# Earlier picking of the p·V sums, a later p·V of pair 14, and transfers in halves, in a decode kernel of four attention layers

## The chip, the cores and the metric

The kernel runs on one core of a Trainium2 chip. The metric is device time in microseconds (us), the median over repeated executions.

## The reference

Four attention layers for one token, with two sets of weights and caches used in turn (A, B, A, B). Cut to what matters:

```python
# Hq = 32 heads, Sk = 8192 keys, Dh = 192, D = 640, all bf16, one query row
def attn(x, k_cache, v_cache, wq, wo):
    q = (x @ wq).reshape(1, 1, 32, 192).transpose(0, 2, 1, 3)
    scores = einsum("bhqd,bhkd->bhqk", q, k_cache) * 192 ** -0.5
    o = einsum("bhqk,bhkd->bhqd", softmax(scores), v_cache)
    return o.transpose(0, 2, 1, 3).reshape(1, 1, 6144) @ wo

x = A_x
for w in (A, B, A, B):
    x = x + attn(layernorm(x), w.k_cache, w.v_cache, w.wq, w.wo)
```

Every K and V cache is read once per layer. A layer needs 32 heads x 8192 keys x 192 x 2 bytes, 100.7 MB of K and as much of V. So the kernel is one long read of the caches, with just enough arithmetic to keep up, and four places where a layer ends and the next one starts.

## The kernel before

A layer works through 16 pairs of heads. K and V of a pair are 6.29 MB each, that is 128 rows of 49,152 bytes. On chip they go into a pool of 8 slots of 24 KB per partition; a whole K or V takes two slots, a half takes one. All loads but that of the input row are issued by one engine (SP) into one queue, in the order of a list called `plan`; each issue waits until the slots that it overwrites have been read. Two more lists matter: `steps` is the order in which the compute work of a layer is written to the engines, and `released` says at which step a slot becomes free. The slot search takes, for each transfer, the slots that become free earliest in `steps`. So moving a step in the program can move a transfer into another slot.

The steps of pair p have one-letter names, which the text uses:

- `m` (products): VectorE multiplies K by the query row, four operations of 1.7 us for each half of K; TensorE sums them with identity matmuls into PSUM.
- `s` (softmax): maximum and exponentials.
- `v` (p·V): TensorE multiplies V by the exponentials. The result lies in PSUM in eight pieces that have to be picked and added.
- `e` (picking, `gather` in the code): VectorE picks and adds the eight pieces, then TensorE and ScalarE write one row of o.
- `wc`, `wo`, `wob`, `wol`: the output projection. `wc` turns the rows of o of five pairs into columns, `wo` multiplies a block of the weights by them. In layers 1 and 3 the last block comes in two transfers (`NB`, `wob`), and `wol` are the rows of the last pair.
- `wq`: query rows of a layer. In layers 2 and 3 they are loaded in three blocks.

Some caches stay on chip: K of pair 0 of layer 0 is kept for layer 2, and V of pairs 14 and 15 of layer 1 for layer 3.

The order of the steps, as the kernel before has it (cut to the lines that the change touches):

```python
            for p in range(NPAIR):
                ...
                steps.append(("m", l, p, 0))
                ...
                if p == NPAIR - 1:
                    steps.append(("v", l, p - 1))      # p.V of pair 14 between the halves of K15
                steps.append(("m", l, p, 1))
                ...
                if p == NPAIR - 1:
                    steps.append(("e", l, p - 1))
                elif p > 0 and p % PAIRS_W > 0 or p > 2 * PAIRS_W:
                    steps.append(("e", l, p - 1))      # picking of p-1 behind the products of p
                steps.append(("s", l, p))
                ...
                if p < NPAIR - 2:
                    ...
                    steps.append(("v", l, p))
                    if p + 1 in (PAIRS_W, 2 * PAIRS_W):
                        b = (p + 1) // PAIRS_W - 1
                        steps += [("e", l, p), ("wc", l, b)]
                        both(("wo", l, b))             # both: into plan and into steps
            ...
            plan.insert(-2, ("wo", l, 2))
            steps += [("wc", l, 2), ("v", l, p, 0), ("wo", l, 2), ("v", l, p, 1)]
            if NB[l]:                                  # NB = [0, 5, 0, 5]
                both(("wob", l))
            steps.append(("e", l, p))
            both(("wol", l))
```

Which transfers come whole, and how a slot is chosen:

```python
        def whole(kind, l, p):
            if kind == "t":
                return False
            if kind == "k":
                return l < 2 or l == 3 and p > 1
            if p == NPAIR - 1:
                return False
            return l != 2 or p not in (PAIRS_W, 2 * PAIRS_W)
        ...
        i = min(range(0, NSLOT - k + 1, 2 if k == 2 else 1),
                key=lambda i: (max(end[i:i + k]), first * i))   # the slots released earliest
```

The picking:

```python
            def gather(p):
                ...
                for i in range(2 if end else VK):      # VK = 8; end: pair 15 has two pieces
                    e = DV.op(lambda v, i=i: (
                        v.tensor_scalar(acc[:], O[:, 0:DH], pick[:, 0:1], None, ALU.mult) if i == 0 else
                        v.scalar_tensor_tensor(out=acc[:], in0=O[:, i * DH:(i + 1) * DH], scalar=pick[:, i:i + 1],
                                               in1=acc[:], op0=ALU.mult, op1=ALU.add)), ...)
```

## Time and profile before

The time before is 1990.04 us, the median of 4 runs (1989.65 to 1991.7).

| what | before |
|---|---|
| span of the profiled execution | 1988.6 us |
| bytes of the load queue | 848.38 MB, 99.3% of 16 DMA engines' span |
| TensorE, VectorE busy | 65%, 60% |
| rate in undisturbed stretches | 432 GB/s |

These lines are from the profile page of the kernel before. The first is the span; the second gives the data rate in 40 equal slices of the span (about 50 us each); the last two are DMA queues, with packets, megabytes and the share of 16 engines' span.

```profile
span 1988.6 us, 14015 instructions
GB/s 411 439 428 431 437 430 430 436 430 428 436 429 436 423 431 436 427 434 430 424 393 435 427 428 434 428 430 430 431 403 430 434 431 435 429 438 428 432 436 342
q1 hardware_dynamic: 25712, 848.38, 99.3%
q8 instruction: 45, 0.74, 0.1%
```

The load queue is nearly always busy, so the kernel is bound by its loads. Slices 21 and 30 (393 and 403 GB/s) are dips, and the first and last slices are start and tail.

The windows of the kernel before show the dips at closer range. The columns are named in the first line: stretch, its length, busy time of each engine with the number of instructions, the TensorE clock that was granted, the share of the DMA engines, and GB/s.

```profile
core 0: us, PE busy (x) PEld busy (x) DVE busy (x) ACT busy (x) POOL busy (x), PEclk, DMA share, GB/s
500.00:985.00 485.00, 306.08 (x1963) 36.85 (x768) 283.59 (x323) 32.65 (x108) 0.55 (x1) 0.76 1.00 432
985.00:1010.00 25.00, 19.14 (x198) 4.89 (x122) 15.16 (x19) 1.89 (x7) 0.00 (x0) 0.84 0.92 379
1010.00:1045.00 35.00, 24.38 (x212) 5.87 (x121) 21.96 (x28) 3.85 (x8) 0.55 (x1) 0.79 1.01 410
1470.00:1512.00 42.00, 29.45 (x283) 8.84 (x206) 17.20 (x23) 2.15 (x8) 0.00 (x0) 0.74 0.93 395
1960.00:1989.00 29.00, 19.82 (x265) 8.78 (x210) 10.44 (x20) 2.15 (x8) 0.00 (x0) 0.72 0.67 285
```

The stretch 500 to 985 us is the plateau. Layer 1 ends and layer 2 begins in the second and third window; layer 2 ends in the fourth; the last is the tail.

The next lines are the timeline of the load queue in the kernel before: start in us, time that the issues took, the line of the program, and what is loaded. `x2` are two issues that the view has merged.

```profile
990.10 9.64 SPq L358 DMA_DIRECT2D pool<-in_B_v_cache_dram  x2
1002.03 0.33 SPq L337 DMA_DIRECT2D rows<-in_B_wo_dram  x1
1029.28 0.34 SPq L358 DMA_DIRECT2D pool<-in_A_k_cache_dram  x1
1037.24 0.33 SPq L356 DMA_DIRECT2D pool<-in_A_v_cache_dram  x1
1488.89 0.80 SPq L358 DMA_DIRECT2D pool<-in_A_v_cache_dram  x2
```

The first line is V of pair 15 in layer 1, whose first half is issued at 990.10 us. The last block issued before it landed at 994.5 us, so at that moment the queue holds 4.4 us of work. The second line is `wol` of layer 1. The third is the first K of layer 2 (pair 1), the fourth its first V. The fifth is V of pair 15 in layer 2: it is issued at 1488.89, just when the p·V step of pair 14 has ended (the timeline has the last matmuls of that step at 1488.25 and 1488.69), and the load before it landed at 1489.3: the queue has run dry.

Why V15 is late in layer 1 shows on VectorE, in the timeline of the kernel before:

```profile
976.26 3.14 DVE L622 SCALAR_TENSOR_TENSOR acc<-OY,small,acc 128x192 f32<-128x192 f32 x7
981.41 13.43 DVE L530 TENSOR_TENSOR pool<-pool,q_sb 128x3072 bf16<-128x3072 bf16 x8
995.54 3.13 DVE L622 SCALAR_TENSOR_TENSOR acc<-OY,small,acc 128x192 f32<-128x192 f32 x7
```

The first line is the picking of pair 13, the second the products of K15, the third the picking of pair 14. The products of K15 stand behind softmax of pair 14 in VectorE's program, and that stands behind the picking of pair 13.

The tail of the kernel before, from its timeline:

```profile
1978.90 2.73 PE L593 MATMUL OY<-pool,p_sb 128*4 128x384 bf16 x32 [3.40 <-DMA pool<-in_B_v_cache_dram]
1981.56 0.38 PE L608 MATMUL TB<-small,ones 128*64 128x1 f32 x4
1981.87 1.16 PE L500 MATMUL OY<-oT,pool 128*128 128x1 bf16 x25
1985.36 0.35 SPq L687 DMA_DIRECT2D out_dram<-x_bf  x1
```

TensorE waits 3.40 us for V15's second half, then has 2.73 us of p·V, the sums of the exponentials, and the last block of the projection. The output is issued at 1985.36.

### The profile page before, as it was taken

How to read it: one execution, taken by the hardware profiler on the slowest of the kernel's cores; microseconds unless marked ns; L12 is line 12 of the kernel's file. 1: busy time of each engine (PE TensorE's matmuls, PEld its weight loads, DVE VectorE, ACT ScalarE, POOL GpSimd, SP SyncE). 2: the span in 40 equal slices, each digit the busy share in tenths (PEclk: the TensorE clock that was granted, in tenths of full speed). 3: DMA queues.
4: the chain of work that ended last, by engine and by line, in shares of the span. 5: the costliest groups of instructions: out<-in, count | busy, mean ns of one | idle time of the engine just before them, and what ended most of it. 6: DMA issues, size and time to landing. Idle time of an engine off the chain costs nothing.

```text
span 1988.6 us, 14015 instructions
## 1 busy us (share of the span) xinstructions
PE 1287.4 (65%) x8310; PEld 156.0 (8%) x3266; DVE 1196.8 (60%) x1371; ACT 139.4 (7%) x461; POOL 4.4 (0%) x22
## 2 busy tenths in 40 slices
PE   3566566667466666566675675675667766666667
PEld 0001001000100100100020010010002001001001
DVE  3466575577157566566754575665764764755656
ACT  0000000000000000000010000000000100000000
POOL 0000000000000000000000000000000000000000
PEclk9787787777587688787777777878877877878777
DMA  9999999999999999999999999999999999999998
GB/s 411 439 428 431 437 430 430 436 430 428 436 429 436 423 431 436 427 434 430 424 393 435 427 428 434 428 430 430 431 403 430 434 431 435 429 438 428 432 436 342
DMA packets 25919, 849.26 MB, mean 427 GB/s; under 512 B 3072, under 2 KB 3072, under 8 KB 3840
## 3 DMA queue, kind: packets, MB, share of 16 engines
q1 hardware_dynamic: 25712, 848.38, 99.3%
q8 instruction: 45, 0.74, 0.1%
q14 instruction: 18, 0.15, 0.0%
q10 hardware_dynamic: 144, 0.00, 0.0%
HBM read 848.36 MB, written 0.00 MB: 427 GB/s over the span
## 4 chain that ended last, share of the span: by engine, by line
DMA 65%; DVE 18%; PE 14%; issue 2%; ACT 1%; SPq 0%
DMA pool<-in_B_k_cache_dram 28%; DMA pool<-in_A_k_cache_dram 19%; DVE pool L530 14%; DMA pool<-in_A_v_cache_dram 14%; PE S L58 5%; PE OY L58 4%; DMA pool<-in_B_v_cache_dram 4%; PE OY L593 3%; DVE acc L622 2%; DMA pool<-in_A_wq_dram 1%; DVE s_sb L552 1%; ACT p_sb L567 1%; PE OY L500 0%; PE S L543 0%; DVE acc L621 0%
## 5 line engine op out<-in xcount | busy, mean ns | idle before, releaser
L530 DVE TENSOR_TENSOR pool<-pool,q_sb 128x3072 bf16<-128x3072 bf16 x512 | 861.6, 1753 | 577.0 <-DMA pool<-in_A_k_cache_dram 288.0
L58 PE MATMUL S<-pool,ident 128*128 128x512 bf16 x2944 | 791.0, 426 | 19.2 <-DVE pool L530 17.3
L543 PE MATMUL S<-pool,ident 128*128 128x512 bf16 x128 | 62.6, 489 | 316.4 <-DVE pool L530 316.4
L593 PE MATMUL OY<-pool,p_sb 128*16 128x512 bf16 (+1 forms) x1216 | 156.2, 541 | 128.2 <-DMA pool<-in_A_v_cache_dram 59.4
L58 PE MATMUL OY<-pool,p_sb 128*16 128x512 bf16 x1920 | 219.1, 547 | 0.0
L622 DVE SCALAR_TENSOR_TENSOR acc<-OY,small,acc 128x192 f32<-128x192 f32 x424 | 177.2, 418 | 14.9
L633 PE MATMUL TB<-acc,small 128*1 128x192 f32 x240 | 58.7, 375 | 134.8 <-DVE acc L622 134.8
L489 ACT ACTIVATE q_sb<-QM 128x192 bf16<-128x192 f32 x60 | 19.8, 330 | 1353.2 <-PE QM L483 1353.2
L552 DVE TENSOR_REDUCE s_sb<-S 128x64 f32<-128x512 f32 x128 | 83.4, 683 | 14.7 <-PE S L58 14.6
L617 DVE RECIPROCAL small<-TB 1x2 f32<-1x2 f32 x64 | 11.2, 175 | 109.8 <-PE TB L604 56.7
L543 PEld LDWEIGHTS S<-pool,ident 128*128 128x128 bf16 x128 | 12.9, 101 | 741.5 <-DVE pool L530 679.2
L593 PEld LDWEIGHTS OY<-pool,p_sb 128*16 128x16 bf16 (+1 forms) x1216 | 37.9, 114 | 332.6 <-issue 225.7
L644 ACT ACTIVATE rows<-TB,small 1x192 bf16<-1x192 f32 x120 | 43.1, 405 | 293.5 <-PE TB L633 272.1
L567 ACT ACTIVATE p_sb<-s_sb,small 64x128 bf16<-64x128 f32 x128 | 55.7, 435 | 55.7 <-DVE small L561 54.2
L557 PE MATMUL QM<-ident,m_bf 128*64 128x64 bf16 x128 | 15.1, 233 | 40.6 <-DVE m_bf L554 39.7
L500 PE MATMUL OY<-oT,pool 128*128 128x1 bf16 x900 | 38.2, 178 | 2.2 <-ACT oT L515 2.2
L500 PEld LDWEIGHTS OY<-oT,pool 128*128 128x128 bf16 x900 | 37.1, 131 | 5.4 <-ACT oT L515 2.9
L483 PEld LDWEIGHTS QM<-rows,one_b 1*64 1x64 bf16 x120 | 6.2, 100 | 350.6 <-issue 344.7
L633 PEld LDWEIGHTS TB<-acc,small 128*1 128x1 f32 x240 | 16.3, 87 | 176.6 <-DVE acc L622 143.6
L561 DVE TENSOR_REDUCE small<-QM 128x1 f32<-128x64 f32 x64 | 14.4, 225 | 23.9 <-PE QM L557 23.6
L621 DVE TENSOR_SCALAR acc<-OY,small 128x192 f32<-128x192 f32 x64 | 26.7, 417 | 1.9
L567 ACT ACTIVATION_READ_ACCUMULATOR p_sb<-s_sb,small 64x1 f32 x128 | 23.3, 182 | 0.0
(59 smaller groups left out, 182.6 us busy)
## 6 DMA issues: line engine op xcount, KB each, us to landing
pool<-in_B_k_cache_dram SPq DMA_DIRECT2D x30, 6144.0 KB, 35.9
pool<-in_A_v_cache_dram SPq DMA_DIRECT2D x28, 6144.0 KB, 25.7
pool<-in_B_v_cache_dram SPq DMA_DIRECT2D x28, 6144.0 KB, 29.5
pool<-in_A_k_cache_dram SPq DMA_DIRECT2D x16, 6144.0 KB, 32.9
pool<-in_A_k_cache_dram SPq DMA_DIRECT2D x30, 3072.0 KB, 20.5
pool<-in_A_v_cache_dram SPq DMA_DIRECT2D x8, 3072.0 KB, 13.2
pool<-in_A_wo_dram SPq DMA_DIRECT2D x6, 2400.0 KB, 20.7
pool<-in_B_v_cache_dram SPq DMA_DIRECT2D x4, 3072.0 KB, 24.9
```

Source lines behind the costliest of these rows:

```text
L58: return t.add_instruction(mybir.InstMatmult(name=t.bass.get_next_instruction_name(), engine=mybir.EngineType.PE, ins=[t.lower_ap(rhs), t. ...
L489: lambda a: a.activation(q_sb[i][:], QM[:, 0:DH], ACT.Copy), e, last["q"][i], bank=QMu)
L500: e = PE.op(lambda t, i=i, c=c, f=y_first[0], fin=n[0] == "wol" and i == k - 1: t.matmul(YB[:, c:c + 1], lhsT=t3[:, i, c:D:DC], rhs=o[:, i ...
L530: e = DV.op(lambda v, d0=d0: v.tensor_tensor(k3[:, :, d0:d0 + QD], kin[:, :, d0:d0 + QD], q_sb[qi][:, d0:d0 + QD].unsqueeze(1).broadcast_t ...
L543: t.matmul(S[:, :], lhsT=ident[:], rhs=k3[:, :, d0:d0 + R], start=True, stop=fin) if d0 == 0 else
L552: lambda v, u=u: v.tensor_reduce(s[:, u * JU:(u + 1) * JU], SP_[u][:].rearrange("p (j r) -> p j r", r=R), AX.X, ALU.add), ev_S[p, u], last ...
L567: ev_p[p] = AC.op(lambda a, h=h, r=r: a.activation(p_sb[par][r, :, h], s[r, :], ACT.Exp, bias=negm[par][r, 0:1], accum_out=l_col[par][r, h ...
L593: t.matmul(o, lhsT=x, rhs=y, start=f, stop=fin) if c == 0 else
L621: v.tensor_scalar(acc[:], O[:, 0:DH], pick[:, 0:1], None, ALU.mult) if i == 0 else
L622: v.scalar_tensor_tensor(out=acc[:], in0=O[:, i * DH:(i + 1) * DH], scalar=pick[:, i:i + 1], in1=acc[:], op0=ALU.mult, op1=ALU.add)), e if ...
L633: e = PE.op(lambda t, h=h: t.matmul(TB[96:97, C_O + h * DH:C_O + (h + 1) * DH], lhsT=half[:, h:h + 1], rhs=acc[:], start=True, stop=True), ...
L644: last["TO"] = last["row_written"] = AC.op(lambda a, h=h: a.activation(orow[:, o0 + h * DH:o0 + (h + 1) * DH], TB[96:97, C_O + h * DH:C_O ...
```

## The change

Its intent is to take the picking off VectorE's way to the next softmax, and to issue loads earlier at the places where the queue runs dry. It has five parts:

1. Picking of a pair directly behind its p·V.
2. p·V of pair 14 behind both halves of the products of pair 15, its picking behind softmax 15. In layer 2 the slot search then gives V15's first half another slot.
3. The first V of layer 2 in halves, and its first half ahead of K of pair 1 in the plan.
4. K in halves behind the `wo` blocks (pairs 5 and 10 of layers 0 and 1).
5. In layers 1 and 3, the last half of V15 in two transfers, the sums of the exponentials (called l columns below) ahead of p·V, and `wc` behind the first half of V15's p·V.

The diff, cut to its core; the repeated declaration of semaphores, and the code that merely moves the l columns up, are left out:

```diff
             if kind == "k":
-                return l < 2 or l == 3 and p > 1
+                return l < 2 and p not in (PAIRS_W, 2 * PAIRS_W) or l == 3 and p > 1
             ...
-            return l != 2 or p not in (PAIRS_W, 2 * PAIRS_W)
+            return l != 2 or p not in (0, PAIRS_W, 2 * PAIRS_W)
 ...
-                if p == NPAIR - 1:
-                    steps.append(("v", l, p - 1))
+                if l == 2 and p == 1:
+                    steps.append(("e", l, 0))
                 steps.append(("m", l, p, 1))
 ...
                 if p == NPAIR - 1:
-                    steps.append(("e", l, p - 1))
-                elif p > 0 and p % PAIRS_W > 0 or p > 2 * PAIRS_W:
-                    steps.append(("e", l, p - 1))
+                    steps.append(("v", l, p - 1))
                 steps.append(("s", l, p))
 ...
                             i = plan.index(("k", l, 1, 0))
-                            plan[i - 2:i + 1] = [("k", l, 1, 0)] + plan[i - 2:i]
+                            plan[i - 1:i + 1] = [("k", l, 1, 0), ("v", l, 0, 1)]
                     steps.append(("v", l, p))
+                    if l != 2 or p > 0:
+                        steps.append(("e", l, p))
                     if p + 1 in (PAIRS_W, 2 * PAIRS_W):
                         b = (p + 1) // PAIRS_W - 1
-                        steps += [("e", l, p), ("wc", l, b)]
+                        steps.append(("wc", l, b))
                         both(("wo", l, b))
 ...
-            steps += [("wc", l, 2), ("v", l, p, 0), ("wo", l, 2), ("v", l, p, 1)]
+            steps.append(("e", l, p - 1))
+            steps += [("v", l, p, 0), ("wc", l, 2)] if NB[l] else [("wc", l, 2), ("v", l, p, 0)]
+            steps += [("wo", l, 2), ("v", l, p, 1)]
             if NB[l]:
+                plan.append(("vq", l))
                 both(("wob", l))
 ...
+                if quarters(n):                      # the last half of V15, layers 1 and 3
+                    x = TS // 2
+                    if n in landed:
+                        return SP.op(lambda s: s.dma_start(t[:, x:], r[:, TS + x:]), sem=semVQ, inc=16)
+                    return SP.op(lambda s: s.dma_start(t[:, 0:x], r[:, TS:TS + x]), *free, sem=semS[i], inc=16)
 ...
-                PE.wait(ev_p[p], last["O"])
+                PE.wait(ev_p[p])
+                if 0 in us:
+                    ...                              # the l columns, formerly behind p.V
+                PE.wait(last["O"])
 ...
+                    if p == NPAIR - 1 and i == rounds // 4 and quarters(("v", nl, np_, u)):
+                        PE.wait(need(("vq", l)))
```

More of the change, by code (lines that the diff above doesn't have):

```diff
@@ L168, in build @@
         semS = [sem(f"semS{i}") for i in range(NSLOT)]
-        semOL, semOB, semX, semOUT = sem("semOL"), sem("semOB"), sem("semX"), sem("semOUT")
+        semOL, semOB, semVQ, semX, semOUT = [sem(n) for n in ("semOL", "semOB", "semVQ", "semX", "semOUT")]
         e = PO.op(lambda g: g.memset(ident[:], 0.0))
@@ L305, in build @@
                 before[n] = [("wc", n[1], 2)]
-            elif n[0] == "wob":
+            elif n[0] in ("wob", "vq"):
                 before[n] = []
@@ L328, in wq_rows, with quarters @@
             return slot[place[("wq", l, g)]][:, 0:k * QC].rearrange("p (c n) -> p c n", c=k)
+        def quarters(n):
+            return n[0] == "v" and n[2:] == (NPAIR - 1, 1) and NB[n[1]] > 0
         def transfer(n):
@@ L347, in transfer @@
                     sem=semOB, inc=16)
+            if n[0] == "vq":
+                n = ("v", l, NPAIR - 1, 1)
             i = place[n]
@@ L577, in values @@
                 N = min(512, k * DH)
-                PE.wait(ev_p[p], last["O"])
+                PE.wait(ev_p[p])
+                if 0 in us:
+                    PE.wait(last["rl"])
+                    if p < NPAIR - 1:
+                        e = PE.op(lambda t: t.matmul(TB[96:97, C_L:C_L + 2], lhsT=ones[:, 0:1], rhs=l_col[par][:],
+                                                     start=True, stop=True), bank=TBu)
+                    else:
+                        for h in range(2):
+                            e = PE.op(lambda t, h=h: t.matmul(TB[64 * h:64 * h + 64, C_L:C_L + 1], lhsT=ones[:, 0:1].broadcast_to([P, 64]),
+                                                              rhs=l_col[par][:, h:h + 1], start=True, stop=True),
+                                      signal=h == 1, bank=TBu)
+                    last["lc"][par] = ev_l[p] = e
+                PE.wait(last["O"])
                 rounds = J // k // G
@@ L601, in values @@
                         freed[("v", nl, np_, u)] = e
-                PE.wait(last["rl"])
-                if p < NPAIR - 1:
-                    e = PE.op(lambda t: t.matmul(TB[96:97, C_L:C_L + 2], lhsT=ones[:, 0:1], rhs=l_col[par][:],
-                                                 start=True, stop=True), bank=TBu)
-                else:
-                    for h in range(2):
-                        e = PE.op(lambda t, h=h: t.matmul(TB[64 * h:64 * h + 64, C_L:C_L + 1], lhsT=ones[:, 0:1].broadcast_to([P, 64]),
-                                                          rhs=l_col[par][:, h:h + 1], start=True, stop=True),
-                                  signal=h == 1, bank=TBu)
-                last["lc"][par] = ev_l[p] = e
             def gather(p):
```

## The prediction

> **What bounds it.** The DMA engines. The page's queue table has the one load queue at 99.3% of 16 engines' span, 848.4 MB. By windows, DMA share is 1.00 at 430 to 432 GB/s in the long stretches (0-500, 500-985, 1060-1470, 1512-1960 us), which is the plateau: whole-pair transfers move at about 432.6 GB/s. The Trainium skill ("DMA: Bandwidth & Descriptors", Specifications) gives 435 GB/s as fabric ceiling; the trace agrees closely. DVE (60%) and PE (65%) have slack. At the plateau 848.4 MB take about 1961 us (estimate), so of 1988.6 us only some 27 us are start, tail and holes.
>
> **Where the holes are** (windows, and the queue's waits against the landings before): 985-1060 us runs at 398 GB/s (about 6 us lost), 1470-1512 at 395 (3.6 us), and behind layer 1's wo blocks (670, 820 us) about 1.1 us. Layers 0 and 3 have none.
>
> **What the change does, costed:**
>
> 1. Picking behind p.V. It is eight DVE operations, 0.42 us each, 3.55 us with the reciprocal. It leaves the path K products -> softmax -> p.V and goes into DVE's wait for K (10 us in layers 0/1). On the plateau this is worth nothing: the queue is backed up by 12 us and more. It pays at the end of layer 1: K15's products start 3.8 us sooner (now 981.4 after the picking at 975.6), so V15's first half is issued at about 986 instead of 990.1, when the queue still has work; its second half is no longer issued 2.65 us before the queue runs dry. Worth 2.2 us.
> 2. V(14) after both product halves in the program. In layer 2 the slot search then gives V15's first half the slot of K15's second half, free at about 1477, not V14's, free at 1488.9. The queue ran dry at 1489. Worth 3.0 us.
> 3. Layer 2's first V in halves, with the kept K's slots first: V no longer waits for the last wq block (issued 1037.2 with 1.5 us of work left). Worth 1.75 us. The hole before it (wq's last block, products of half 0; 1.3 us) stays.
> 4. K in halves behind wo: the first half takes a slot free already, margin 4.7 -> over 10 us. Worth 1.1 us in layer 1, nothing in layer 0 (no hole there).
> 5. V15's last half in two: behind the last landing 16 p.V matmuls instead of 32 (2.73 us); the l columns (0.3 us) go ahead. The last wo rows then set the pace, so the tail shrinks by about 1.0 us, once, in layer 3; in layer 1 it starts layer 2 sooner.
> 6. Cost: halves move at 430.2 instead of 432.6 GB/s: 0.4 us.
>
> Layer 3 has 20 us and more queued, so what is gained earlier arrives at the end.
>
> Sum: 2.2+3.0+1.75+1.1+1.0-0.4 = 8.6 us. **Predicted 1981.5 us, 1978.5 to 1986.0 in 8 of 10.** Faster by over 2%: 0; within: 0.99; slower: 0.01.
>
> **In the profile.** Right: bytes, DVE and PE busy times unchanged; slice rates near 393 and 403 GB/s rise above 415; window 1470-1505 at 425 or more; first slices unchanged; from the last V landing to the end 1 us less. Step 1 is wrong if V15's first half in layer 1 is still issued within 5 us of the queue's end; step 2 if a wait of the load queue on p.V of pair 14 still leaves a hole; step 3 if layer 2's first V waits for wq.
>
> **What would make it wrong.** DVE waiting in order for p.V (5.1 us at the lower clock) before K's products: in layer 2 they start about 1.7 us later; if margins of 9 to 12 us are eaten, new holes come. A new hole at layer 2's start, where wq's blocks follow one another. Or engines' skew (up to 4.7 us) that returns as loss.

## The result and the profile after

The kernel after takes 1985.61 us, the median of 4 runs (1985.17 to 1986.01). The ratio to the kernel before is 0.9976, with a 95% interval of 0.9959 to 0.9993. A ratio is the mean time of one kernel's runs over that of the other's of the same rounds, so it is not quite the ratio of the medians. The gain is 4.4 us by the medians. A second measurement of the same kernel, below, gave a ratio of 0.9971.

The page of the kernel after, the same lines as before:

```profile
span 1984.0 us, 13908 instructions
GB/s 412 438 430 431 431 437 429 431 430 431 433 435 431 432 429 436 430 431 432 427 388 433 430 430 430 432 430 430 431 431 427 435 432 434 430 432 432 432 431 353
q1 hardware_dynamic: 26720, 848.38, 99.5%
```

The bytes are the same. The dip of slice 30 has gone (403 before, 431 now). The dip of slice 21 has not: 393 before, 388 now.

The windows of the kernel after, with the columns as before:

```profile
500.00:985.00 485.00, 299.06 (x1975) 35.09 (x776) 288.28 (x325) 32.86 (x109) 0.55 (x1) 0.76 1.00 432
985.00:1010.00 25.00, 18.58 (x207) 5.65 (x142) 12.09 (x18) 1.89 (x7) 0.00 (x0) 0.82 0.95 395
1010.00:1045.00 35.00, 26.61 (x226) 5.53 (x111) 17.32 (x24) 3.86 (x8) 0.55 (x1) 0.74 0.95 391
1470.00:1512.00 42.00, 28.40 (x289) 10.17 (x222) 14.99 (x31) 2.15 (x8) 0.39 (x1) 0.69 1.00 424
1960.00:1989.00 29.00, 15.09 (x235) 8.53 (x199) 5.39 (x16) 2.15 (x8) 0.00 (x0) 0.67 0.56 230
```

(The rate is a mean over the 16 DMA engines.) Before, the 25 us at the end of layer 1 ran at 379 GB/s and the 35 us at the start of layer 2 at 410. Now they run at 395 and 391. Worked out, the 60 us carry 23.8 MB before and 23.6 MB after. As a mean of the engines the hole has not been closed; it has moved by 25 us. In the fourth row, at the end of layer 2, the rate rises from 395 to 424, and that gain stays.

The load queue's timeline after:

```profile
987.05 0.33 SPq L371 DMA_DIRECT2D pool<-in_B_v_cache_dram  x1
1006.66 0.33 SPq L343 DMA_DIRECT2D rows<-in_B_wo_dram  x1
1029.60 0.34 SPq L371 DMA_DIRECT2D pool<-in_A_v_cache_dram  x1
1478.96 10.08 SPq L371 DMA_DIRECT2D pool<-in_A_v_cache_dram  x2
```

V15's first half is issued at 987.05 instead of 990.10, as intended. But the first load of layer 2's caches (now a half of V) starts at 1029.60, against 1029.28 before. At the end of layer 2, V15's first half is issued at 1478.96, ten microseconds sooner than before.

VectorE at the end of layer 1, after:

```profile
978.17 13.43 DVE L543 TENSOR_TENSOR pool<-pool,q_sb 128x3072 bf16<-128x3072 bf16 x8
996.95 3.14 DVE L639 SCALAR_TENSOR_TENSOR acc<-OY,small,acc 128x192 f32<-128x192 f32 x7
```

K15's products start 3.2 us sooner (978.17, was 981.41), now with no picking ahead of them: that of pair 13 has gone. The picking of pair 14 stood behind them before too (995.54); it is now behind softmax 15 as well, at 996.95.

The tail after:

```profile
1968.70 2.73 PE L620 MATMUL OY<-pool,p_sb 128*4 128x384 bf16 x32
1974.80 2.73 PE L620 MATMUL OY<-pool,p_sb 128*4 128x384 bf16 x32
1977.74 1.16 PE L513 MATMUL OY<-oT,pool 128*128 128x1 bf16 x25 [0.21 <-DMA pool<-in_B_wo_dram]
1981.22 0.35 SPq L704 DMA_DIRECT2D out_dram<-x_bf  x1
```

p·V of V15 no longer ends the chain: the projection that follows waits 0.21 us for the second transfer of the last block of wo (`wob`), and from there to the output is 3.5 us.

### Where the time went, as a ledger

The following table is worked out from the DMA records of the traces, in the program's order of transfers; it is not a view of the profile. It cuts an execution at fixed points: (a) the last `wo` block of layer 1 issued ahead of V15 has landed; (b) from there until the `wol` rows of layer 1 have landed; (c) until the first packet of the first K or V transfer of layer 2; (d) until the first `wo` block of layer 2 has landed; (e) until the last one has; (f) until the last `wq` block of layer 3 has; (g) until the last load; (t) from there to the end of the span.

```
                       a      b      c       d       e      f       g     t    span
before              994.5  18.61  17.11  139.60  319.49  50.60  441.60  7.07  1988.6
after               995.1  17.77  17.74  138.88  319.09  47.86  442.01  5.58  1984.0
after, second time  994.5  17.78  17.51  139.24  318.94  47.89  441.94  6.16  1984.0
only V14            994.0  18.03  17.89  140.09  318.84  48.00  442.66  8.21  1987.7
only picking        994.3  20.25  17.13  142.16  319.17  50.53  441.53  6.86  1991.9
only last half      993.9  19.39  18.68  140.81  319.88  49.49  441.82  5.97  1989.9
V14 and last half   994.4  19.32  16.82  141.14  318.84  48.11  442.55  7.58  1988.8
picking put back    994.3  19.13  19.35  138.96  319.24  47.94  442.75  8.16  1989.8
wc first            994.4  17.82  17.37  140.26  318.53  48.70  441.99  5.97  1985.0
K whole             994.1  17.81  17.37  139.66  318.62  48.28  441.53  6.31  1983.7
first V whole       994.4  17.79  17.39  139.88  318.94  48.00  441.66  5.92  1984.0
warm                994.5  17.80  16.98  139.10  319.11  47.71  441.87  5.99  1983.1
products first      994.5  17.79  16.62  142.56  319.14  48.14  441.57  5.58  1985.9
products, wc first  994.5  17.81  15.44  142.93  318.81  48.04  441.61  5.55  1984.7
```

The first two rows give the result: of 4.6 us, 2.7 come from the end of layer 2 (f) and 1.5 from the tail (t). The end of layer 1 (b) gives 0.8, the start of layer 2 (c) takes 0.6 back. One execution of each kernel stands in each row, so differences of a few tenths should not be read. The two largest terms hold in the other rows too: f is 49.5 to 50.6 us in the three rows without V14's move and 47.7 to 48.7 in the eleven with it.

### The profile page after: what moved, and what is told of

Its sections match the earlier page's. It is cut to its first block, busy times and chain, and to the rows that moved or that the text cites. A ratio compares the mean times of both kernels' runs of the same rounds, so it can differ in the third digit from the quotient of the medians.

```text
span 1984.0 us, 13908 instructions
## 1 busy us (share of the span) xinstructions
PE 1273.4 (64%) x8310; PEld 150.1 (8%) x3266; DVE 1200.7 (61%) x1371; ACT 139.5 (7%) x461; POOL 4.5 (0%) x22
## 4 chain that ended last, share of the span: by engine, by line
DMA 68%; DVE 15%; PE 15%; ACT 1%; issue 0%; SPq 0%
DMA pool<-in_B_k_cache_dram 27%; DMA pool<-in_A_v_cache_dram 20%; DMA pool<-in_A_k_cache_dram 14%; DVE pool L543 13%; PE S L58 6%; PE OY L58 5%; DMA pool<-in_B_v_cache_dram 4%; PE OY L620 3%; DMA pool<-in_B_wo_dram 2%; ACT p_sb L580 1%; DVE acc L639 1%; DMA pool<-in_A_wq_dram 1%; DVE s_sb L565 1%; PE OY L513 0%; PE S L556 0%
## 5 line engine op out<-in xcount | busy, mean ns | idle before, releaser
L58 PE MATMUL S<-pool,ident 128*128 128x512 bf16 x2944 | 789.1, 425 | 20.3 <-DVE pool L543 19.0
L650 PE MATMUL TB<-acc,small 128*1 128x192 f32 x240 | 82.1, 493 | 219.1 <-DVE acc L639 219.1
L58 PE MATMUL OY<-pool,p_sb 128*16 128x512 bf16 x1920 | 197.0, 485 | 0.0
L620 PE MATMUL OY<-pool,p_sb 128*16 128x512 bf16 (+1 forms) x1216 | 147.5, 497 | 62.7 <-DMA pool<-in_A_v_cache_dram 56.4
L565 DVE TENSOR_REDUCE s_sb<-S 128x64 f32<-128x512 f32 x128 | 88.1, 688 | 69.4 <-PE S L58 69.4
L595 PE MATMUL TB<-small,ones 128*1 128x2 f32 x120 | 11.4, 165 | 74.1 <-ACT p_sb L580 74.1
## 6 DMA issues: line engine op xcount, KB each, us to landing
pool<-in_B_k_cache_dram SPq DMA_DIRECT2D x28, 6144.0 KB, 38.1
```

The source lines that it names most:

```text
L58: return t.add_instruction(mybir.InstMatmult(name=t.bass.get_next_instruction_name(), engine=mybir.EngineType.PE, ins=[t.lower_ap(rhs), t. ...
L565: lambda v, u=u: v.tensor_reduce(s[:, u * JU:(u + 1) * JU], SP_[u][:].rearrange("p (j r) -> p j r", r=R), AX.X, ALU.add), ev_S[p, u], last ...
L620: t.matmul(o, lhsT=x, rhs=y, start=f, stop=fin) if c == 0 else
L650: e = PE.op(lambda t, h=h: t.matmul(TB[96:97, C_O + h * DH:C_O + (h + 1) * DH], lhsT=half[:, h:h + 1], rhs=acc[:], start=True, stop=True), ...
```

## The experiments

Twelve runs were made, one of them of the kernel after again, all with five rounds, all correct within the reference's tolerance. The kernel before: medians 1991.57, 1990.72, 1991.06 and 1991.44 us. It scatters more than the kernel after: 1988.62 to 1996.02 in 36 executions.

Two theories stood against each other after the first reading:

- **Theory A, the last engine.** A transfer is split over 16 DMA engines, and it has landed when the last of them is done. I had counted a hole in the queue as the mean idle time of the 16. If the engines are spread out in time, a short hole idles those in front and not the last one, and costs little.
- **Theory B, the late `wc`.** The change puts `wc` of layers 1 and 3 behind V15's first half. `wol` is then issued at 1006.66 instead of 1002.03. This opens a new hole that eats the gain.

The expectations of the first two runs below also call "theory B" the prediction's own reckoning, that every hole is worth its mean over the engines.

The spread can be read from the DMA records. The first and the last engine finish the last `wo` block of layer 1 at 990.57 and 994.52 us before, and at 988.34 and 995.07 after. The Trainium skill ("DMA: Bandwidth & Descriptors", section "Why a DMA increments its semaphore by 16 and not by 1") says that a transfer runs on up to 16 engines that finish independently, and that only the full count of 16 means that all data has landed. The trace agrees: the spread at that block is 4.0 us before and 6.7 after, and yet the block's landing moves by no more than 1.2 us over all 14 profiled executions (993.9 to 995.1).

### Each part alone

**Only V14's move** (part 2). Edit of the kernel before:

```diff
-                if p == NPAIR - 1:
-                    steps.append(("v", l, p - 1))
                 steps.append(("m", l, p, 1))
                 if p == NPAIR - 1:
-                    steps.append(("e", l, p - 1))
+                    steps.append(("v", l, p - 1))
 ...
             plan.insert(-2, ("wo", l, 2))
+            steps.append(("e", l, p - 1))
             steps += [("wc", l, 2), ("v", l, p, 0), ("wo", l, 2), ("v", l, p, 1)]
```

> The kernel before with one part of the change: V14's p.V stands behind both product halves of pair 15 and its picking behind that softmax. Theory A (a hole in the load queue costs only what it costs the DMA engine that is last; engines are up to 4 to 7 us apart): the hole at the end of layer 2 (1489 us) reached all engines, so this part alone gives 2.5 to 3.5 us. Theory B (every hole is worth its mean over the engines, as in the prediction): 3.0 us as well; this run does not part them, it sizes the term. V15's first half in layer 2 should be issued about 10 us before the queue runs dry instead of 0.4.

Measured: 1989.68 us (1989.28 to 1991.04), ratio 0.9989 (0.9975 to 1.0002): about 2 us, not quite clear of the noise. The ledger's column f falls from 50.6 to 48.0 us, as it was meant to: V15's first half of layer 2 is issued at 1481.68, 7 us ahead of the end of the queue. But the tail grows from 7.07 to 8.21 us. The move puts the picking of pair 14 behind softmax 15, in front of p·V of pair 15, and at the end of a layer nothing hides it.

**Only the picking** (part 1), for pairs up to 13:

```diff
+                if l == 2 and p == 1:
+                    steps.append(("e", l, 0))
                 steps.append(("m", l, p, 1))
 ...
-                elif p > 0 and p % PAIRS_W > 0 or p > 2 * PAIRS_W:
-                    steps.append(("e", l, p - 1))
 ...
                     steps.append(("v", l, p))
+                    if l != 2 or p > 0:
+                        steps.append(("e", l, p))
 ...
```

> The kernel before with the picking moved directly behind p.V and nothing else. Prediction (theory B): 2.2 us from the end of layer 1. Theory A: at most 0.5 us, because the engine that was last had no hole there, and the start of layer 2 is timed by its own chain (first wq block landed, query row, products of the kept K, slot free at about 1029 us).

Measured: 1993.65 us (1989.57 to 1995.22), ratio 1.0004 (0.9991 to 1.0016): nothing. V15's first half in layer 1 is issued at 987.24, as forecast. Its second half is issued at 1000.88, when only 0.7 us is left in the queue, and column b is 20.25 instead of 18.61 us. In this order p·V of pair 14 stands between the two halves of K15's products on TensorE, so the sums of the second half, which free that slot, still wait for V14. One wait was taken away and the next one took its place. It even cost something: TensorE now stood idle for 3.87 us before p·V of pair 14, and the step took 4.5 us (991.08 to 995.56) instead of 2.8; the clock record has half the clock granted from 991.2 to 994.6, and the full clock at that place in the kernel before.

**Only the last half in two** (part 5 without the move of `wc`); the edit is the `quarters`, `vq` and l-column lines of the diff above.

> The kernel before with V15's last half in two transfers in layers 1 and 3 and the l columns ahead of p.V. Both theories: 1.0 to 1.5 us less, all of it between the last landing and the end; time from the last p.V landing to the end about 1.4 us shorter in the profile.

Measured: 1991.3 us (1989.67 to 1992.49), ratio 0.9993 (0.9981 to 1.0006). In the profile the tail is 5.97 us instead of 7.07, so the 1.0 us of the forecast is there. In the times it does not show: b and c together are 38.1 us here and 35.7 in the kernel before. Whether that is scatter or an effect of this part, one profile can't say.

**V14's move and the last half together**, that is the first and third of these edits in one kernel:

> The kernel before with only two of the parts: V14 behind both product halves, and the tail (V15's last half in two, l columns ahead). Theory A: these two carry the gain, 3 to 4 us below before. Theory B: the other three parts (picking, K in halves, first V in halves) add their 5 us, so it stays 4 to 5 us short of after, that is at before.

Measured: 1988.0 us (1987.67 to 1990.65), ratio 0.9989 (0.9976 to 1.0001). By the medians that is 3.1 us below the kernel before, by the means 2.4. The profiled execution was the slowest of the five, so its span (1988.8) is not typical. This is short of the whole change (0.9971 to 0.9976), though the intervals overlap. It suggests that some part that is missing here matters, although picking alone is worth nothing.

### One part taken out of the kernel after

**`wc` first again:**

```diff
-            steps += [("v", l, p, 0), ("wc", l, 2)] if NB[l] else [("wc", l, 2), ("v", l, p, 0)]
+            steps += [("wc", l, 2), ("v", l, p, 0)]
```

> The kernel after with the wo columns put back ahead of V15's first half in layers 1 and 3 (as the kernel before had it). Theory B: the change lost its gain at the end of layer 1 to this later place (wq of layer 2 issued at 1007.0 instead of 1002.4 us), so about 1.5 to 2 us faster than after. Theory A: only engines that are ahead idle there, so within 0.5 us of after, although wq's issue moves back to about 1003 us.

Measured: 1986.55 us (1985.55 to 1986.78), ratio 0.9970 (0.9957 to 0.9982), the same as the kernel after. These are the two windows of this kernel at the end of layer 1 and the start of layer 2, columns as before:

```profile
985.00:1010.00 25.00, 19.02 (x217) 5.89 (x158) 11.97 (x18) 1.89 (x7) 0.00 (x0) 0.86 0.99 417
1010.00:1045.00 35.00, 25.37 (x214) 5.15 (x99) 17.31 (x24) 3.85 (x8) 0.55 (x1) 0.76 0.95 387
```

Here the hole at the end of layer 1 is closed: 417 GB/s, against 395 after and 379 before. And it gains nothing. The start of layer 2 falls only from 391 to 387, and the 60 us carry 24.0 MB, against 23.6 after and 23.8 before; but the 0.4 MB, worth about 1 us, do not reach the time: column b of the ledger, which goes by the last engine, is 17.82 us here and 17.77 after. Theory B forecast 1.5 to 2 us for this run and is not borne out as the reason for the missing microseconds of the kernel after.

**K whole behind wo** (part 4 out):

```diff
-                return l < 2 and p not in (PAIRS_W, 2 * PAIRS_W) or l == 3 and p > 1
+                return l < 2 or l == 3 and p > 1
```

> After, with K behind the wo blocks of layers 0 and 1 whole again. Prediction and theory B: 1.1 us slower than after (the holes at 673 and 826 us come back, about 0.5 us of idle time as mean of the engines). Theory A: within 0.5 us of after, because the engine that is last (4 to 6 us behind the first) has no hole there, and what is saved there is lost at the start of layer 2.

Measured: 1985.5 us (1985.02 to 1987.42), ratio 0.9971 (0.9957 to 0.9984). The kernel after in the same rounds:

> The kernel after, unchanged, as the reference for the runs of this call on the same chip. 1985 to 1987 us.

It took 1985.84 us (1984.57 to 1987.57), ratio 0.9971 (0.9959 to 0.9984). So no gain of K in halves shows. The intervals alone, about 2.6 us to either side, could not exclude the 1.1 us of the forecast, but the records show why there is none. K of pair 5 in layer 1 is issued 4.7 us before the last engine is done with the block before it, and its first packet follows the issue by 0.96 us; the engines are spread over 4.1 us at that point. The leading engine does stand idle for a while: from its end of the block before to its end of K it takes 15.3 us. The last one takes 14.54 us for the same 6.29 MB, which is 432.7 GB/s, as on the plateau. After this block the spread is smaller, 3.3 us, and the loss is no loss at all. Theory A holds here.

**First V of layer 2 whole** (part 3 out):

```diff
-            return l != 2 or p not in (0, PAIRS_W, 2 * PAIRS_W)
+            return l != 2 or p not in (PAIRS_W, 2 * PAIRS_W)
 ...
-                            plan[i - 1:i + 1] = [("k", l, 1, 0), ("v", l, 0, 1)]
+                            plan[i - 2:i + 1] = [("k", l, 1, 0)] + plan[i - 2:i]
```

> After, with layer 2's first V whole and behind wq's last block again. Prediction and theory B: 1.75 us slower than after. Theory A: 0.3 to 1 us slower, as the hole behind it reaches all engines but costs what is left after the one before it; and more scatter from run to run, since the kernels with a whole V there (before 1990 to 1996 us, picking alone 1990 to 1995) scatter and after (1984.6 to 1987.6) does not.

Measured: 1987.16 us (1985.51 to 1990.93), ratio 0.9982 (0.9970 to 0.9995), against 0.9971 and 0.9976 of the kernel after. The profiled execution has the same span as the kernel after, 1984.0. In the ledger's column d the six kernels with the first V whole have 139.6 to 142.2 us, and the six with halves and the order of the kernel after 138.9 to 140.3. This kernel's own 139.88 stands against 138.88 and 139.24 of the two profiles of the kernel after. But two other kernels with halves have 140.26 and 139.66, on either side of it, and the intervals of the runs overlap. So a gain from the halves is not shown; if there is one, it is about a microsecond.

**Picking put back behind the next pair's products** (part 1 out, the rest in):

```diff
                 if p == NPAIR - 1:
                     steps.append(("v", l, p - 1))
+                elif (p > 0 and p % PAIRS_W > 0 or p > 2 * PAIRS_W) and (l, p) != (2, 1):
+                    steps.append(("e", l, p - 1))
 ...
                     steps.append(("v", l, p))
-                    if l != 2 or p > 0:
-                        steps.append(("e", l, p))
                     if p + 1 in (PAIRS_W, 2 * PAIRS_W):
                         b = (p + 1) // PAIRS_W - 1
-                        steps.append(("wc", l, b))
+                        steps += [("e", l, p), ("wc", l, b)]
```

> After, with the picking back behind the next pair's products; everything else of the change stays. Prediction for this part: 2.2 us slower than after (V15's first half in layer 1 issued at about 991 us again). By subtraction from the runs so far (two parts alone 2.4 us below before, all five 5.0 to 5.6, K in halves 0, first V in halves about 1.5) some 1 to 1.5 us are left for it. Theory A in its strict form says 0.5 us at most, since the last engine's landing at the end of layer 1 is the same in all kernels so far (994 to 995 us for the last wo block).

Measured: 1992.01 us (1989.12 to 1992.65), ratio 1.0002 (0.9988 to 1.0015). Theory A in its strict form said that the picking is worth at most half a microsecond, because the last engine hardly had a hole. Instead the whole gain is gone, and the interval does not touch that of the kernel after in its measurement of five rounds (0.9959 to 0.9984). The picking that was worth nothing when it was added alone cannot be taken out. (Both are compared through the kernel before.)

The lines of this kernel's timeline, first VectorE and the queue at the end of layer 1 (picking 13, products of K15, picking 14, `wol`), then TensorE and the queue in the tail:

```profile
975.98 3.13 DVE L639 SCALAR_TENSOR_TENSOR acc<-OY,small,acc 128x192 f32<-128x192 f32 x7
981.13 13.43 DVE L543 TENSOR_TENSOR pool<-pool,q_sb 128x3072 bf16<-128x3072 bf16 x8
999.91 3.13 DVE L639 SCALAR_TENSOR_TENSOR acc<-OY,small,acc 128x192 f32<-128x192 f32 x7
1009.51 0.33 SPq L343 DMA_DIRECT2D rows<-in_B_wo_dram  x1
```

```profile
1974.28 2.73 PE L620 MATMUL OY<-pool,p_sb 128*4 128x384 bf16 x32
1980.37 2.73 PE L620 MATMUL OY<-pool,p_sb 128*4 128x384 bf16 x32
1986.52 0.35 SPq L704 DMA_DIRECT2D out_dram<-x_bf  x1
```

Picking 14 in layer 1 runs at 999.91, in the kernel after at 996.95; `wol` is issued at 1009.51 against 1006.66; the first transfer of layer 2 has its first packet at 1032.75 against 1030.58. A delay of 3 us runs down one chain of compute and comes out at the other end as 2.2. In the tail, p·V of V15's first half starts at 1974.28 against 1968.70: 2.6 us after its data had landed here, 0.3 us in the kernel after. The last load lands at 1981.64, but p·V ends at 1983.1: the tail is bound by compute now, and takes 8.16 us instead of 5.58. The difference of the two spans, 5.8 us, is 2.6 us of tail, 2.2 us at layer 2's start (its first packet), and 1.0 us in small sums over the rest.

My reading is that the moves belong together. V14's move frees a slot in layer 2, at the price of one picking behind softmax 15 at the end of every layer. Moving the other picking away from in front of K15's products pays that price. But there is a rival. This kernel also has `wc` late, and the kernel with V14 and the last half alone, which kept 2 to 3 us without the picking's move, has not; that one loses less at layer 2's start (column c, 16.82 against 19.35). The two timelines show the difference: there `wol` is issued at 1006.95; here p·V of V15's first half stands ahead of `wc` for 2.7 us, and `wol` is issued at 1009.51. So the late `wc` may be what the picking has to make room for, but no run has tested this by itself.

### What sets the start of layer 2

Column b has a floor. In all eight kernels with picking and V14's move together it is 17.77 to 17.82 us. Between (a) and the `wol` rows the queue moves 6.29 + 0.82 + 0.49 = 7.60 MB; in 17.8 us that is 427 GB/s, as much as rows of this size were seen to get. The kernel before needed 18.61. So by the last engine only 0.8 us was ever to be had at the end of layer 1, and all of it was won. What follows is column c, about 17 us from there to layer 2's first transfer, and the change does not make it shorter. Two things run in it. One is a chain of compute: the projection, the sum over the row, the query row, the products of K0, and their sums, which free the slot. The other is the queue itself: in this time it moves the three `wq` blocks, 7.37 MB, and these alone take about 17.3 us (an estimate from the 426 GB/s at which rows of 11,520 bytes moved in these traces). So column c is nearly all transfer as well. What the chain of compute costs can be bounded: from the `wol` rows to the landing of the first half of layer 2's caches the kernel after takes 26.1 us in both profiles and the kernel before 25.6, while the transfers alone need about 24.6 (the same estimate, with 430 GB/s for the half). So about 1.5 us are lost there after and 1.0 us before, in single executions; the rest of the dip in the windows is idle time of the leading engines.

This is TensorE in the timeline of the kernel after, at that place:

```profile
1020.28 0.59 PE L481 MATMUL OY<-pool,xb 128*1 128x512 bf16 x3 [2.21 <-DMA pool<-in_A_wq_dram]
1023.98 5.59 PE L58 MATMUL S<-pool,ident 128*128 128x512 bf16 x23
1029.50 0.38 PE L481 MATMUL OY<-pool,xb 128*1 128x512 bf16 x3
```

TensorE waits for the first block of `wq` until 1020.28 (1020.60 before), spends 3.3 us on query rows, then 5.6 us on the sums of K0's first half, and at 1029.60 the slot is free and the transfer is issued. Three runs tried to shorten this.

**Products first:** the sums of K0's first half ahead of the query rows, and the last `wq` block behind V:

```diff
-                plan += [("wq", l, g) for g in range(3)]
-                steps.append(("wq", l, 0))
+                plan += [("wq", l, g) for g in range(2)]
 ...
                 if l == 2 and p == 0:
-                    steps.append(("wq", l, 1))
+                    steps.append(("wq", l, 0))
 ...
                 if l == 2 and p == 0:
-                    steps.append(("wq", l, 2))
+                    steps += [("wq", l, 1), ("wq", l, 2)]
 ...
-                            plan[i - 1:i + 1] = [("k", l, 1, 0), ("v", l, 0, 1)]
+                            plan[i - 1:i + 1] = [("wq", l, 2), ("k", l, 1, 0), ("v", l, 0, 1)]
```

> After, with the start of layer 2 taken apart: the products of the kept K's first half are summed on TensorE before the query row's first block, and V's first half is issued ahead of wq's last block. Theory A (what was saved up to the end of layer 1 is lost at one point, the chain wq block landed - query row - products - slot free, at 1029.6 us): V's first half is issued at about 1025.5 us, while wq's second block still moves, the hole of 2.4 us at 1020 to 1040 us is gone, and the time falls by 2 to 3 us against the kernel after. Theory B (the later wo columns ate the gain): they are as late as in after, so at most 1 us.

Measured: 1987.6 us (1986.56 to 1987.84), ratio 0.9979 (0.9966 to 0.9991). It is a miss: no gain, rather a loss of a microsecond or two against the kernel after in the same rounds (0.9971). The sums and the queue in its timeline:

```profile
1020.10 7.82 PE L58 MATMUL S<-pool,ident 128*128 128x512 bf16 x23
1027.95 0.34 SPq L370 DMA_DIRECT2D pool<-in_A_v_cache_dram  x1
1029.67 0.34 SPq L375 DMA_DIRECT2D pool<-in_A_wq_dram  x1
```

The 23 sums took 7.82 us, where they take 5.1 to 5.6 in the other kernels. The granted clock was half until 1025.5 us, and up to there most started 427 ns apart; the last nine followed 216 ns apart. In the kernel after the half clock lasts about as long (to 1024.9), but there the query rows run in it first. V's first half was issued at 1027.95, 0.9 us sooner than in the kernel after of the same rounds. But the edit had taken the last `wq` block, 1.47 MB or 3.4 us of work, from ahead of V. The block before it was done at 1026.13, V's first packet came at 1028.91, and in between all 16 engines stood dry for 2.8 us, where the kernel after has 0.2 to 0.3. That is why this run is a miss: the block that was moved away had covered the wait. It landed at 1040.8 us, against 1029.6, and column d grew to 142.56 us.

**Products first with `wc` first** (both edits):

> The same with the wo columns ahead of V15's first half in layers 1 and 3. Theory A: within 0.7 us of the run with products first alone. Theory B: at least 1.5 us below it.

Measured: 1986.9 us (1986.16 to 1988.46), ratio 0.9978 (0.9965 to 0.9990). Column c is the shortest of all, 15.44 us, and column d the longest, 142.93, since the last `wq` block has moved from one into the other. All engines stand dry for 1.6 us before V (1026.12 to 1027.76). Again what is won at one place is paid at the next.

**Warm:** the kernel after with 12 spare matmuls (into a PSUM bank that is overwritten afterwards) placed where TensorE waits: two behind picking 15 of layer 1, one behind its `wol`, one behind the sums of the layernorm, and eight behind the first query row.

```diff
+        def warm(k):
+            PE.wait(ev_first[0], *last["S"])
+            for i in range(k):
+                PE.op(lambda t: t.matmul(SP_[1][:], lhsT=ident[:], rhs=wq0[0][:].rearrange("p c n -> p (c n)")[:, 0:512],
+                                         start=True, stop=True), signal=False)
```

> After, with 12 spare 512-column matmuls (into a bank that is overwritten next, results unused) in TensorE's waits between layer 1's last product and layer 2's query row. In after the row's first block takes 3.3 us for 24 matmuls and the products' sums 5.9 us, against 1.6 and 5.3 us where TensorE has been busy. If the hole at 1020 to 1040 us comes from TensorE being slow right after its waits (theory A, sharpened), the first block takes about 2 us or less, V's first half is issued near 1027.5 us instead of 1028.9 to 1029.6, and the time falls by 1 to 2 us. If the hole comes from the landing of wq alone, nothing changes.

Measured: 1985.21 us (1984.46 to 1986.60), ratio 0.9973 (0.9959 to 0.9986). Its span in the profile, 1983.1 us, is the shortest, but the times do not set it apart from the kernel after. The spare matmuls and the query rows of this kernel:

```profile
1017.89 3.44 PE L432 MATMUL S<-wq,ident 128*128 128x512 bf16 x8
1021.26 0.38 PE L492 MATMUL OY<-pool,xb 128*1 128x512 bf16 x3
```

The effect itself is there. The query rows of the first block took 1.7 us (1021.26 to the start of the sums at 1022.98) instead of 3.3. But the eight spare matmuls took 0.43 us each, ran past the landing of the `wq` block, and gave most of it back. The Trainium skill ("TensorE: Matmul & The Clock Gate", Part 1, "Wait — 56ns, not 53.3ns?") gives 426.7 ns for such a matmul on a cold array and 215.7 on a warm one. The trace agrees: 0.43 us here, 223 ns in the 23 sums that follow. A version with four spare matmuls instead of eight was not run.

No kernel beats the kernel after by more than the scatter.

## Why the prediction was right or wrong

The time, 1985.61 us, lies inside the range of 1978.5 to 1986.0, 0.4 us below its upper end, and "within 2%" was right. That it lies inside is in part luck: three of the five gains in the sum came out far smaller or not at all, and the range was 7.5 us wide. What bounds the kernel was right: the loads, at 432 GB/s on the plateau. The Trainium skill's figure that the prediction used ("DMA: Bandwidth & Descriptors", Specifications: 435 GB/s) fits, since rows of 49,152 bytes moved at 432.6. The gain, however, was to be 8.6 us and was 4.4 by the medians (4.9 in the second measurement). Step by step:

1. **Picking, "Worth 2.2 us".** This step failed. The transfer was issued earlier as forecast (987.05, forecast "about 986"), but the sizing took the mean idle time of the 16 engines. By the last engine there were 0.8 us (column b), and column c took 0.4 to 0.6 of them back. The forecast that the slice near 393 GB/s would rise above 415 failed (388). Alone the step was worth nothing, and yet without it the whole gain is gone. The prediction said that it pays through the hole at the end of layer 1; as the timelines of the run with the picking put back read, it pays by taking 2.3 to 3 us out of the chain of compute at the ends of layers, which V14's move, or the late `wc`, or both had made longer.
2. **V14's move, "Worth 3.0 us".** Right in mechanism and nearly in size: column f fell by 2.7 us in the kernel after and by 2.6 with the move alone. The window 1470 to 1512 rose from 395 to 424 GB/s; in the forecast's own window, 1470 to 1505, it is 422, a little short of the 425 that was named. What the prediction did not cost was its price: the tail is 1.1 us longer with the move alone.
3. **First V of layer 2 in halves, "Worth 1.75 us".** The order is as forecast, since V no longer waits for the last `wq` block. But the term was too large: column d fell by 0.4 to 0.7 us in the whole change, and with the part taken out no loss clear of the scatter was seen. The prediction named a possible new hole at layer 2's start; the first transfer there did not come sooner (first packet 1030.24 before, 1030.58 and 1029.83 after), and the loss at that place, about 1.0 us before, is about 1.5 us after.
4. **K in halves, "Worth 1.1 us in layer 1".** This failed: no gain, as the run with K whole and its records show. The hole was there in the mean of the engines, but the last engine had none.
5. **The last half in two, "about 1.0 us".** Right: 1.1 us in the profile with the part alone, 0.9 to 1.5 in the kernel after.
6. **Cost of halves, "0.4 us".** It cannot be told from the other terms. Column g is 0.3 to 0.4 us longer, but it lies in layer 3, where of the added cuts there is only the one in V15's last half.

The failing terms of the sum are 2.2, 1.1 and 1.75, together 5.05 us, in place of which the ledger shows 0.2 (b and c together), −0.6 (a) and 0.7 (d) in the first profile, and 0.4, 0 and 0.4 in the second. The prediction had named the spread of the engines, "up to 4.7 us", as what could make it wrong, and still sized three of its steps as though there were none. It also added the parts as though they were independent. The runs show that they are not: V14 with the last half gave 2 to 3 us, picking alone 0, all together 4.4 to 4.9, and everything but the picking 0.

What stays open: whether the V halves gain anything, whether the late `wc` is what makes the kernel without the picking so slow at layer 2's start, and why the orders of the parts alone scatter in column b (18.0 to 20.3 us) beyond the one cause that was read for the picking.

## What to carry to other kernels

In this kernel a hole in the load queue cost what the last DMA engine lost, not the mean of the engines: compare how long before the queue's end the next load is issued with the spread of the engines at that place plus the time from issue to first packet (1 us here), and expect nothing from closing a hole that only the leading engines see. At the seam between two layers, ask for each stretch whether the loads in it already fill it: where they nearly did, loads issued earlier only moved the leading engines' hole to the other side of the seam, and a load taken out of the stretch opened a real one. So read both sides before crediting a gain. Test the parts of a change both by adding one alone and by taking one out; here one part was worth nothing alone and the whole gain in company.

## What the Trainium skill lacked or had wrong

- "Runtime: NRT & Kernel Launch", section "Instruction fetch mechanics", says that instruction memory is refilled in blocks of 16 KiB through a DMA queue of the sequencer, and that the fetch is mostly hidden. The trace agrees on the blocks: 45 instruction packets of 16,384 bytes. It lacks what they cost the loads: a packet takes about 1.06 us on one of the 16 engines that also carry the loads (at 118.9 us of the execution, before, the load packets of one engine show a gap of 1.03 us around it), and that engine falls behind by so much. A gap of 0.98 to 1.16 us stands behind each of the first 20 of them. In a backed-up queue the first and the last engine drift apart, from 1.7 us at 172 us of the execution to 4.7 us at 675 us (before) and 6.7 us at 992 us (after). I put the drift down to these packets; no run has tested it.
- "DMA: Bandwidth & Descriptors" says that the engines finish independently, but not that their spread decides what a hole in a queue costs. Here a load issued 4.7 us before the queue's end, at a spread of 4.1 us, cost nothing that shows against one issued far ahead (ratio 0.9971 both).
- The same page has no rates for rows above 4 KiB on this path, loads issued from SP. Seen here, worked out from the median time of a row's packet, for 16 engines: 432.6 GB/s with rows of 49,152 bytes, 430.2 with 24,576 and 425.6 with 12,288.
